# Four blocks for batch 0, swapped operands for the last 192 tokens, and output rows of 2 KB in a fused Fourier-mixing and mixture-of-experts kernel

## The chip, the cores and the metric

One core of a Trainium2 chip (trn2). The metric is the time of one execution on the device in microseconds (us), lower is better. Each kernel is timed in several executions; a run of the kernel before stands in the same rounds on the same chip. All runs quoted are fast, with a mean granted TensorE clock of 0.99 to 1.00. A profile shows one single execution: for the changed kernels one of the timed ones, for the kernel before a further one.

## The reference

Eight batches of 2496 tokens with 256 channels pass through a Fourier mixing layer; then each batch goes as a whole to one of eight experts.

```python
X = np.fft.rfft(x, axis=1)                     # x: 8 x 2496 x 256
Yr = Xr @ w_r - Xi @ w_i + b_r                 # complex 256x256 mixing
Yi = Xr @ w_i + Xi @ w_r + b_i
Y  = soft_threshold(Yr, 0.01) + 1j * soft_threshold(Yi, 0.01)
y  = np.fft.irfft(Y, n=2496, axis=1)
# mixture of experts, one expert e for a whole batch
e   = argmax(y.mean(axis=1) @ w_gate)
out = gate_weight * (np.maximum(y @ w1[e], 0) @ w2[e])   # 256 -> 1024 -> 256
```

## The kernel before

The transform of 2496 = 39 x 64 points is done by matmuls in two steps. A token index is 64 a + n, with a below 39 and n below 64. Everything is issued in a fixed order: a small list scheduler written in Python runs while the kernel is built. It takes operations in order of a priority `vt` and of its own estimates of durations and arrivals, and emits each to its engine. Every engine of the chip is thus given its list in a fixed order. So an estimate or a priority never delays anything by itself, but it decides what stands in front of what.

Cuts marked with `# ...`:

```python
class Schedule:
    def mm(self, cols, emit, vt, deps=(), allocs=(), after=None): ...   # a TensorE op
    def evac(self, n, emit, vt, deps=(), allocs=()): ...  # PSUM eviction: ScalarE or VectorE, chosen by the scheduler
    # an op waits for deps and for the earlier users of the buffers in allocs

apool = pool("ap", 1)             # ONE buffer for the tile A
opool = pool("op", 4)             # output tiles, 128 x 2 x 256 fp32
BANKS = {"a": 4, "h": 2, "o": 2}  # PSUM banks

# batch 0: its spectrum V is built inside the A buffer, then turned by TensorE in six pieces
VTk = S.tok("A", 1)
def add_turn(v_ops, vt):
    for gq in range(6):
        # ...  8 matmuls against an identity, out of the A buffer
        m = S.mm([128] * (2 * len(gs)), mm, vt(0.8 + 0.02 * gq), ...)
        VTk.rel.append(m)         # A is free after the last turn matmul
        # ...  one eviction of 1024 columns

# batches 2 to 7: the first step of the forward transform also writes A
Ak = S.tok("A", 1)
m = S.mm([512], mm, vt(-0.2 + 0.01 * gp), ..., allocs=[tk] if gp else [tk, Ak])
# ... then A -> DRAM -> XB (a transposing round trip), and the mixing starts from XB

# batch 0: inverse in six pieces, all of them needed by the first MoE matmul
for gb in range(6):
    va = vt(0.9 + 0.02 * gb)
    # ...  8 matmuls, one eviction of 936 columns into ysb

NCH = [(0, 512), (512, 512), (1024, 512), (1536, 512), (2048, 448)]
def add_moe(b, y_ops, yk, gate):
    for c, (ns, nl) in enumerate(NCH):
        for fc in range(E):       # 8 pieces of the hidden layer
            # two matmuls of nl columns, then a relu eviction of nl columns
            m = S.mm([nl, nl], mm, v, deps=y_ops + [w], ...)
        for sp in range(2):       # two pairs of output tiles, each 128 tokens x 256
            s0 = min((2 * sp + i) * P, nl - P)   # the last tile of 448 overlaps by 64
            nc.tensor.matmul(oc["p"][:, i, :],               # 16 per pair
                             cell["hs"][:, ft, s0 : s0 + P],   # tokens are the weights
                             w2s_t[b][:, ft, :], ...)          # 256 columns move
            # eviction with the gate's scale, store on the sync queue in rows of 1 KB
```

The first four chunks of batch 7 use a Strassen product; the change does not touch it.

Of the kernel before, what the change touches and what calls it, by code (L numbers as in the profile page):

```python
# [11 lines left out]
FP32 = mybir.dt.float32  # L12
# [23 lines left out]
def _tables():  # L36
# [22 lines left out]
    wi = wi.reshape(6, NK1, 117)  # L59
    wi0 = wi.transpose(1, 0, 2).reshape(120, 117)  # L60
    wi = np.concatenate([wi[:, k0:k9].reshape(-1, 117) for k0, k9 in PARTS])
# [74 lines left out]
class Schedule:  # L136
# [60 lines left out]
    def run(self):  # L197
        free = dict.fromkeys(("PE", "ACT", "DVE", "SP", "POOL"), 1.3)
        free["PE"], free["ACT"], free["SP"], free["POOL"] = 3.85, 4.0, 3.5, 6.0
        ring = {"SP": 17.5, "POOL": 26.0}  # L200
        todo = sorted(self.ops, key=lambda o: o.vt)
# [47 lines left out]
def kernel(  # L249
# [114 lines left out]

    X0_AT, X1_AT = (5.2, 7.6, 9.4, 10.8), 26.5
    W_AT = 11.6
    TF_AT, TI_AT = (12.3, 14.4, 16.4), (13.2, 15.4, 17.4)

# [9 lines left out]
    WARM, COLD, WARM_END = 60, 12, 11.9  # L378
    LATE = -0.12
    FAST = {(B - 1, c) for c in range(4)}  # L380
# [130 lines left out]
    def add_inverse_b(b, q, cell, oy, vt, wide):  # L511
# [38 lines left out]
        return o  # L550

    VTk = S.tok("A", 1)
    S.preset(VTk)
# [41 lines left out]
    def add_turn(v_ops, vt):  # L595

        V2k = S.tok("V2", 2)
        t_ops = []
        for gq in range(6):
            gs = range(4 * gq, min(4 * gq + 4, NG))  # L600
            tag = "oh"[gq % 2]
            tk = S.tok(tag, BANKS[tag], 2)
            hc = {}

            def mm(_, gq=gq, gs=gs, tag=tag, hc=hc):
                if gq == 0:
                    V2_t[0] = v2pool.tile([120, NG, D], FP16, name="V2")
                hc["p"] = pair(tag)
                pt = hc["p"].rearrange("p h c -> p (h c)")
                for i, g in enumerate(gs):  # L610
                    for ch in range(2):
                        c0 = D * i + P * ch
                        nc.tensor.matmul(  # L613
                            pt[0:120, c0 : c0 + P],
                            first["T"][:, ch, g], eye)
            m = S.mm([128] * (2 * len(gs)), mm, vt(0.8 + 0.02 * gq),
                     deps=v_ops + [small], after=t_ops[-1] if t_ops else None,
                     allocs=[tk] if gq else [tk, V2k])
            VTk.rel.append(m)

            def ev(eng, gs=gs, hc=hc):
                n = len(gs)
                src = hc["p"].rearrange("p h c -> p (h c)")
                COPY[eng](out=V2_t[0][:, gs[0] : gs[0] + n].rearrange(
                    "p g c -> p (g c)"), in_=src[0:120, 0 : D * n])
            e = S.evac(D * len(gs), ev, vt(0.8 + 0.02 * gq), deps=[m])
            tk.rel.append(e)
            t_ops.append(e)
        return t_ops, V2k
# [322 lines left out]
    def add_inverse_a(b, v_ops, vt):  # L952
# [31 lines left out]
        if b == 0:  # L984
            yk, y_ops = S.tok("ysb", 2), []
            for gb in range(6):
# [4 lines left out]
                def mm(_, gs=gs, cell=cell):  # L991
                    if gs[0] == 0:
                        ysb_t[b] = ypool.tile([P, 2, N], FP16, name="ysb")
                    cell["p"] = pi = pair("a")
                    for ch in range(2):
                        for i, g in enumerate(gs):
                            M = 39 if g == 21 else 117
                            nc.tensor.matmul(
                                pi[:, ch, 117 * i : 117 * i + M],
                                V2_t[0][:, g, ch * P : ch * P + P],  # L1000
                                wi0[:, 0:117:3] if g == 21 else wi0)
                cols = ([117] * len(gs) if gb < 5 else [117, 39]) * 2
                va = vt(0.9 + 0.02 * gb)
                m = S.mm(cols, mm, va, deps=[r_ops[gb]],
# [4 lines left out]
                def ev(eng, gb=gb, cell=cell):  # L1009
                    yv = ysb_t[b].rearrange("p h (a n) -> p h a n", n=N2)  # L1010
                    nf = 4 if gb < 5 else 1
                    pi = cell["p"]
                    COPY[eng](  # L1013
                        out=yv[:, :, :, 12 * gb : 12 * gb + 3 * nf].rearrange(
                            "p h a (g j) -> p h a g j", j=3),
                        in_=pi[:, :, 0 : 117 * nf].rearrange(
                            "p h (g a j) -> p h a g j", g=nf, j=3))
                    if gb == 5:
                        COPY[eng](out=yv[:, :, :, 63], in_=pi[:, :, 117:156])
                e = S.evac(936 if gb < 5 else 480, ev, va, deps=[m])  # L1020
                tk.rel.append(e)
# [4 lines left out]
        for gb in range(6):  # L1026
            gs = range(4 * gb, min(4 * gb + 4, NG))
            for ch in range(2):
# [3 lines left out]
                def mm(_, gs=gs, ch=ch, cell=cell):  # L1032
# [4 lines left out]
                    for i, g in enumerate(gs):  # L1037
# [7 lines left out]
                va = (vt(0.9 + 0.02 * gb) if b < 1  # L1045
                      else (b + LATE + 0.01 * gb) * PERIOD)
                m = S.mm(cols, mm, va,
# [102 lines left out]

    NCH = [(0, 512), (512, 512), (1024, 512), (1536, 512), (2048, 448)]

# [123 lines left out]
    T_t = {}  # L1276

    def add_moe(b, y_ops, yk, gate):
        w, gb_op, wk = gate
        v0 = b * PERIOD  # L1280
        if any(x == b for x, _ in FAST):
            t_op = add_weight_sums(b, w, wk, v0 - 0.05 * PERIOD)
        for c, (ns, nl) in enumerate(NCH):
            hk = S.tok("hs", BUFS["hs"])
            cell = {}
            h_ops = []
            for fc in range(E):
                v = v0 + PERIOD * (c * 8 + fc) / 44
                tag = "h" if b < B - 1 else "a"
# [3 lines left out]
                def mm(_, fc=fc, ns=ns, nl=nl, cell=cell, hc=hc, tag=tag):  # L1293
# [5 lines left out]
                    for ch in range(2):  # L1299
# [3 lines left out]
                            start=(ch == 0), stop=(ch == 1))  # L1303
                m = S.mm([nl, nl], mm, v, deps=y_ops + [w], after=m if fc else None,
                         allocs=[tk] if fc else [tk, hk])
# [12 lines left out]
            if (b, c) in FAST:  # L1318
                add_fast(b, c, ns, nl, cell, h_ops, hk, wk, t_op, gb_op, v0)
                continue  # L1320
            for sp in range(2):
                tago = "o" if b < B - 1 else "h"
                ok = S.tok(tago, BANKS[tago])
                last = b == B - 1 and c == 4 and sp == 1
                ok2 = S.tok(tago, BANKS[tago])
                oc = {}
                for q in range(4):
                    v = v0 + PERIOD * (c * 8 + 6 + 4 * sp + q) / 44

                    def mm(_, sp=sp, q=q, nl=nl, cell=cell, oc=oc, tag=tago,  # L1330
                           last=last):
                        if q == 0 or q == 2 and last:
                            oc["p"] = oc["p", q // 2] = bank(tag).rearrange("p (i c) -> p i c", i=2)
                        i = q // 2
                        s0 = min((2 * sp + i) * P, nl - P)
                        for ft in range(4 * (q % 2), 4 * (q % 2) + 4):
                            nc.tensor.matmul(  # L1337
                                oc["p"][:, i, :],
                                cell["hs"][:, ft, s0 : s0 + P],
                                w2s_t[b][:, ft, :],  # L1340
# [9 lines left out]

                def ev(eng, oc=oc):
                    oc["o"] = ost = opool.tile([P, 2, D], FP32, name="ost")
                    if eng == "ACT":
                        nc.scalar.activation(out=ost, in_=oc["p"],  # L1354
                                             func=AFT.Copy, scale=gbc_t[b])
                    else:
                        nc.vector.tensor_scalar_mul(out=ost, in0=oc["p"],
                                                    scalar1=gbc_t[b])

                def st(_, ns=ns, nl=nl, sp=sp, oc=oc):  # L1360
                    ost = oc["o"]
                    r0 = ns + 256 * sp
                    if 256 * sp + 256 <= nl:
                        nc.sync.dma_start(
                            out=out[b, r0 : r0 + 256, :].rearrange(
                                "(i p) c -> p i c", p=P),
                            in_=ost)
                    else:
                        nc.sync.dma_start(out=out[b, r0 : r0 + P, :],
                                          in_=ost[:, 0, :])  # L1370
                        nc.sync.dma_start(out=out[b, r0 + P : ns + nl, :],
                                          in_=ost[64:P, 1, :])

                def ev_last(_, ns=ns, nl=nl, sp=sp, oc=oc):
# [3 lines left out]
                    nc.scalar.activation(  # L1378
                        out=ost[64:P, 1], in_=oc["p", 1][64:P, 1],
                        func=AFT.Copy, scale=gbc_t[b][64:P])  # L1380
                    nc.scalar.dma_start(out=out[b, r0 + P : ns + nl, :],
                                        in_=ost[64:P, 1, :])

                def ev_first(_, ns=ns, sp=sp, oc=oc):
# [3 lines left out]
                        out=ost[:, 0], in0=oc["p", 0][:, 0], scalar1=gbc_t[b])  # L1388
                    nc.sync.dma_start(out=out[b, r0 : r0 + P, :],
                                      in_=ost[:, 0, :])  # L1390
                if last:
# [4 lines left out]
                else:  # L1396
                    e = S.evac(560, ev, v, deps=[m2, gb_op])
                    ok.rel.append(e)
                    S.op("SP", 0.3, st, v, deps=[e], dma=0.75)

# [34 lines left out]
```

## Time and profile before

| | before |
|---|---|
| time | 434.88 us median (434.28 to 435.47) |
| span of the profile | 433.1 us |
| matmul work in it (columns/2.4 GHz + 2.5 ns for each matmul) | 408.1 us |
| idle TensorE up to 50 us / from 60 to 150 us | 18.9 us / 0.5 us |
| end of the last matmul / from there to the end of the span | 429.3 us / 3.8 us |

The page of the kernel before, its head, its DMA queues and its chain of waits:

```profile
span 433.1 us, 9390 instructions
PE 419.6 (97%) x3553; PEld 312.2 (72%) x3553; DVE 300.8 (69%) x614; ACT 333.0 (77%) x643; POOL 35.4 (8%) x57
...
q1 hardware_dynamic: 68262, 57.41, 48.3%
q0 software_dynamic: 17216, 18.70, 28.5%
...
PE 89%; DMA 5%; ACT 3%; POOL 1%; SPq 1%; issue 0%; DVE 0%; ACTq 0%; POOLq 0%
```

PE is TensorE, and it holds 89% of the chain. Its busy time is a union of spans whose ends are modelled, so a full slice can still hide small waits. This document therefore also counts work: for every matmul record its columns divided by 2.4 GHz, plus 2.5 ns. The Trainium skill, "TensorE: Matmul & The Clock Gate", section "Back-to-back issue gap", gives N/2.4 + 2.5 ns as the gap of a warm, isolated matmul of N columns. The trace agrees with it for matmuls in a stream too: 109 ns from start to start at 256 columns, 216 ns at 512. "Idle" below is elapsed time less the work of all matmuls started so far, without the warm-up dummies. It contains the wait for the first data, and it would contain time at a lower clock. The last matmul is taken to end one such gap after its start, 0.1 us before its modelled end in the trace.

The stretches view of the kernel before (start:end, length, then busy us and count for each engine, granted clock, DMA share, GB/s):

```profile
31.00:50.00 19.00, 17.04 (x193) 12.73 (x194) 15.85 (x26) 17.78 (x30) 0.00 (x0) 1.00 0.73 103
60.00:70.00 10.00, 10.00 (x66) 6.46 (x65) 6.58 (x12) 8.62 (x17) 0.00 (x0) 1.00 0.76 229
70.00:80.00 10.00, 10.00 (x78) 7.25 (x76) 4.43 (x7) 7.86 (x16) 0.00 (x0) 1.00 1.08 257
80.00:90.00 10.00, 10.00 (x86) 7.74 (x84) 8.02 (x23) 7.06 (x15) 2.45 (x4) 1.00 0.76 157
100.00:150.00 50.00, 50.00 (x420) 38.14 (x418) 38.88 (x79) 38.57 (x78) 4.22 (x6) 1.00 0.89 207
```

From 60 us on TensorE (first number after the length) is full. From 31 to 50 us it shows 17.04 of 19, and the matmuls started there hold only 14.9 us of work; ScalarE (fourth) is busy 17.78. The start is where time is lost. Of 2.3 us of TensorE waits that the profile lists from 25 to 50 us, 2.0 name ScalarE or VectorE, so evictions limit it for the most part.

The chain of waits, one place that returns with the period of a batch:

```profile
187.09 0.46 PE ps L527 x4
...
237.23 0.46 PE ps L527 x4
```

One batch takes 50.14 us. Of the lines, L613 holds the turn matmuls of batch 0 and L793 forward matmuls, those of batch 2 among them. The last turn matmul frees the A buffer that L793 then writes:

```profile
42.33 0.39 PE L613 MATMUL ps<-eye,A 128*120 128x128 f16 x4
...
45.54 0.38 PE L793 MATMUL ps<-xin,wa 117*120 117x512 f16 x1 [0.43 <-ACT ysb L1013]
...
62.50 0.38 PE L793 MATMUL ps<-xin,wa 117*120 117x512 f16 x1
```

And the end of the span:

```profile
425.67 3.77 PE L1337 MATMUL ps<-w2s,hs 128*128 128x256 f16 x32
...
429.47 0.47 ACT L1378 ACTIVATE ost<-ps,gbc 64x256 f32<-64x256 f32 x1 [1.12 <-PE ps L1337]
429.97 0.55 ACTq L1381 DMA_DIRECT2D out_dram<-ost  x1
```

The last store is issued by 430.52 and the span ends at 433.1: 2.6 us for that store to land.

### The profile page before, as it was taken

The page shows a single profiled execution, that of the slowest core. Times are in us where ns is not written, and L with a number is a line of the kernel's source. Part 1 is how long each engine was busy: PE and PEld are TensorE (multiplying, and loading weights), DVE is VectorE, ACT ScalarE, POOL GpSimd, SP SyncE. Part 2 cuts the span into 40 slices and gives each one's busy share as a digit, 9 for nine tenths or more (in the row PEclk, how much of TensorE's full clock was granted, in tenths as well). Part 3 has the DMA queues.
Part 4 walks back from the last instruction along what each step waited for, and adds up shares of the span by engine and source line. Part 5 has one row for each costly group of instructions (what it writes and reads, how often), then busy time and mean ns, then how long its engine had stood idle before and what let it go on. Part 6 is the DMA issues. An engine that isn't in the chain of part 4 may idle for free.

```text
span 433.1 us, 9390 instructions
## 1 busy us (share of the span) xinstructions
PE 419.6 (97%) x3553; PEld 312.2 (72%) x3553; DVE 300.8 (69%) x614; ACT 333.0 (77%) x643; POOL 35.4 (8%) x57
## 2 busy tenths in 40 slices
PE   5888999999999999999999999999999999999996
PEld 2456567778777877778777877778777787777775
DVE  1488866577977787786977878777877869513561
ACT  3789987688876877678867888678777788678884
POOL 5230100011002000021001100020000010000000
PEclk9999999999999999999999999999999999999999
DMA  8899197999895997879995998959987285521122
GB/s 153 224 181 148 33 248 230 200 174 206 208 280 121 226 197 206 248 140 239 180 243 183 194 205 214 284 103 226 207 215 236 87 160 129 182 88 68 50 99 92
DMA packets 85785, 76.96 MB, mean 178 GB/s; under 512 B 7673, under 2 KB 72695, under 8 KB 85740
## 3 DMA queue, kind: packets, MB, share of 16 engines
q1 hardware_dynamic: 68262, 57.41, 48.3%
q0 software_dynamic: 17216, 18.70, 28.5%
q8 instruction: 28, 0.46, 0.5%
q10 hardware_dynamic: 262, 0.25, 0.2%
q14 instruction: 17, 0.14, 0.1%
HBM read 57.54 MB, written 37.49 MB: 219 GB/s over the span
## 4 chain that ended last, share of the span: by engine, by line
PE 89%; DMA 5%; ACT 3%; POOL 1%; SPq 1%; issue 0%; DVE 0%; ACTq 0%; POOLq 0%
PE ps L1300 30%; PE ps L1337 29%; PE ps L895 9%; DMA xin<-in_x_dram 4%; PE ps L1040 4%; PE ps L527 3%; PE ps L793 3%; PE ps L857 3%; PE ps L1219 2%; PE ps L699 2%; ACT hs L1312 1%; DMA tf<-d_tf 1%; PE ps L613 1%; PE ps L732 0%; POOL xin L321 0%
## 5 line engine op out<-in xcount | busy, mean ns | idle before, releaser
L1312 ACT ACTIVATE hs<-ps 128x512 f16<-128x512 f32 (+1 forms) x293 | 168.2, 594 | 68.6 <-PE ps L1300 64.7
L1300 PE MATMUL ps<-ysb,w1s 128*128 128x512 f16 (+1 forms) x640 | 178.4, 374 | 0.1
L1337 PE MATMUL ps<-w2s,hs 128*128 128x256 f16 x1152 | 162.4, 272 | 0.1
L1337 PEld LDWEIGHTS <-hs 128*128 128x128 f16 x1152 | 110.8, 98 | 42.7 <-issue 0.2
L1300 PEld LDWEIGHTS <-w1s 128*128 128x128 f16 x640 | 68.6, 113 | 18.8 <-issue 0.6
L909 DVE TENSOR_TENSOR tt<-ps,bias 128x512 f16<-128x512 f32 x60 | 38.6, 686 | 24.5 <-PE ps L895 24.5
L937 DVE TENSOR_TENSOR Y<-z,cl 64x512 f16<-64x512 f16 x120 | 50.4, 420 | 2.8
L895 PE MATMUL ps<-w,XT 128*128 128x256 f16 x360 | 49.4, 273 | 0.0
L1354 ACT ACTIVATE ost<-ps,gbc 128x512 f32<-128x512 f32 x65 | 44.8, 689 | 2.3 <-PE ps L1337 2.3
L895 PEld LDWEIGHTS <-XT 128*128 128x128 f16 x360 | 35.2, 98 | 7.7
L918 DVE TENSOR_TENSOR z<-ps,tt 128x512 f16<-128x512 f32 x60 | 38.4, 681 | 0.1
L803 ACT CAST A<-ps 120x512 f16<-120x512 f32 x48 | 29.5, 614 | 7.0 <-PE ps L793 6.6
L1056 DVE CAST ysb<-ps 128x468 f16<-128x468 f32 (+1 forms) x24 | 15.0, 629 | 25.6 <-PE ps L1040 25.5
L1056 ACT CAST ysb<-ps 128x468 f16<-128x468 f32 (+1 forms) x60 | 28.0, 523 | 3.2 <-PE ps L1040 2.6
L865 DVE CAST XT<-ps 128x512 f16<-128x512 f32 x24 | 16.5, 688 | 16.0 <-PE ps L857 16.0
L534 ACT CAST V<-ps 128x512 f16<-128x512 f32 x44 | 25.7, 609 | 0.0
L793 PE MATMUL ps<-xin,wa 117*120 117x512 f16 x66 | 23.1, 380 | 0.4 <-ACT ysb L1013 0.4
L534 DVE CAST V<-ps 128x512 f16<-128x512 f32 x26 | 17.9, 688 | 6.5 <-PE ps L527 5.4
L1040 PE MATMUL ps<-wi,V 120*128 120x117 f16 (+1 forms) x308 | 22.4, 214 | 0.0
L865 ACT CAST XT<-ps 128x512 f16<-128x512 f32 x36 | 22.0, 615 | 0.0
L527 PE MATMUL ps<-Y,ti 128*128 128x256 f16 x140 | 21.8, 272 | 0.0
L1040 PEld LDWEIGHTS <-V 120*128 120x128 f16 x308 | 19.8, 98 | 2.4
(104 smaller groups left out, 415.0 us busy)
## 6 DMA issues: line engine op xcount, KB each, us to landing
out_dram<-ost SPq DMA_DIRECT2D x72, 256.0 KB
xin<-in_x_dram POOLq DMA_DIRECT2D x21, 429.0 KB, 11.3
scr<-V SPq DMA_DIRECT2D x35, 256.0 KB
XB<-fwd SPq DMA_DIRECT2D x30, 256.0 KB
V<-scr SPq DMA_DIRECT2D x14, 504.0 KB
fwd<-A SPq DMA_DIRECT2D x18, 360.0 KB
w1s<-in_moe_w_dram POOLq DMA_DIRECT2D x8, 512.0 KB, 7.1
w2s<-in_moe_w_dram POOLq DMA_DIRECT2D x8, 512.0 KB, 8.9
```

The costliest lines, as they stand in the source:

```text
L534: COPY[eng](out=hc["V"][:, n * u : n * u + n].rearrange("p i c -> p (i c)"), in_=hc["p", u])
L865: COPY[eng](out=cell["X"][:, ch, :, 0:2].rearrange("p a r i k -> p a i r k"), in_=hc["p"].rearrange("p (a i r k) -> p a i r k", a=2, i=2, ...
L895: nc.tensor.matmul(pm[:, D * a : D * a + D], cell["X"][:, ch, a, t].rearrange("p i k -> p (i k)"), w4[:, ch, t, :], start=(ch == 0), stop= ...
L909: nc.vector.tensor_add(out=cell["tt"][:, r], in0=cell["T", 2].rearrange("p (a c) -> p a c", a=2), in1=bias[:, r].unsqueeze(1).to_broadcast ...
L918: nc.vector.tensor_add(out=cell["z"][:, r], in0=cell["T", 1 - r].rearrange("p (a c) -> p a c", a=2), in1=cell["tt"][:, r])
L937: nc.vector.tensor_sub(out=Y[64 * r : 64 * r + 64, :, i], in0=cell["z"][s, r], in1=cell["cl"][s, r])
L1040: nc.tensor.matmul(pi[:, 117 * i : 117 * i + M], V2[:, g, ch * P : ch * P + P], w)
L1056: COPY[eng](out=yv[:, :, 12 * gb : 12 * gb + 3 * nf].rearrange("p a (g j) -> p a g j", j=3), in_=pi[:, 0 : 117 * nf].rearrange("p (g a j) ...
L1300: nc.tensor.matmul(ph[:, 0:nl], w1v[:, ch, fc // 4, :, fc % 4], ysb_t[b][:, ch, ns : ns + nl], start=(ch == 0), stop=(ch == 1))
L1312: nc.scalar.activation(out=o, in_=i, func=AFT.Relu)
L1337: nc.tensor.matmul(oc["p"][:, i, :], cell["hs"][:, ft, s0 : s0 + P], w2s_t[b][:, ft, :], start=(ft == 0), stop=(ft == E - 1))
L1354: nc.scalar.activation(out=ost, in_=oc["p"], func=AFT.Copy, scale=gbc_t[b])
```

## The change

Its intents: start batch 0's MoE before its whole inverse transform is done; save the 64 tokens that are computed twice in each last chunk; write longer rows to memory.

1. Batch 0's tokens are laid out in four blocks of 16 values of n. MoE on the first block needs two of the six inverse pieces. The later pieces, and the turn pieces that feed them, are deferred.
2. The last 192 tokens of batches 1 to 7 are computed with operands swapped: w2 is the weight, 192 token columns move. The result is channel by token, so VectorE transposes it in 32 x 32 squares, and GpSimd (the queue that also casts inputs) stores it in rows of 256 B.
3. Output tiles take alternate tokens, so that two neighbouring tokens (2 KB) lie in one partition.
4. New expected arrival times, and an earlier priority for batch 1's inverse (`LATE1`).

```diff
-    X0_AT, X1_AT = (5.2, 7.6, 9.4, 10.8), 26.5
+    X0_AT, X1_AT = (5.2, 8.4, 10.0, 11.35), 30.5          # and others of this kind
-    LATE = -0.12
+    LATE, LATE1 = -0.12, -0.4
+    Y_AT = {2: 2.0, 3: 9.0, 4: 16.0, 5: 20.0}
@@ add_turn
-            m = S.mm([128] * (2 * len(gs)), mm, vt(0.8 + 0.02 * gq),
+            va = vt(0.8 + 0.02 * gq) if gq < 2 else Y_AT[gq] - 1.5
+            m = S.mm([128] * (2 * len(gs)), mm, va,
@@ inverse of batch 0
-                va = vt(0.9 + 0.02 * gb)
+                va = vt(0.9 + 0.02 * gb) if gb < 2 else Y_AT[gb]
@@ chunks: start, length, tiles as (start, tokens per partition), 0 = swapped
-    NCH = [(0, 512), (512, 512), (1024, 512), (1536, 512), (2048, 448)]
+    YB = 16 * N1
+    Y_NEED = {0: 2, 1: 3, 2: 4, 3: 6}
+    NCH0 = [c for r in range(4) for c in (
+        (YB * r, 256, ((0, 2),)), (YB * r + 256, 368, ((0, 2), (240, 1))))]
+    NCH = [(512 * c, 512, ((0, 2), (256, 2))) for c in range(4)] + [
+        (2048, 448, ((0, 2), (256, 0)))]
@@ add_turned (new)
+                    nc.tensor.matmul(
+                        oc["p"][:, h],
+                        w2s_t[b][:, ft].rearrange("p (m h) -> p h m", h=2)[:, h],
+                        cell["hs"][:, ft, s0:nl], ...)
+        e = S.evac(2 * n, ev, v, deps=[m, gb_op])
+            nc.vector.transpose(...)
+            for q in range(4):
+                nc.gpsimd.dma_start(out=ov[q], in_=...)      # rows of 64 fp32
@@ add_moe
+            order = [*enumerate(tiles)]
+            if b == B - 1 and c == 4:
+                order = order[::-1]
+            for sp, tile_s in order:
+                if not tile_s[1]:
+                    add_turned(..., v0 + PERIOD * (x + 6 * nl / 512 + 4 * sp) / 44)
+                    continue
...
-                                cell["hs"][:, ft, s0 : s0 + P],
+                                cell["hs"][:, ft, slice(s0 + i, s0 + n * P, n)],
-                                "(i p) c -> p i c", p=P),
+                                "(p i) c -> p i c", i=2),
```

## The prediction

> **What bounds it now.** Per slice, TensorE is busy without a gap from 50 to 422 us (stretches view: 50.00 of 50.00 in every period); the chain of waits is 89% TensorE, and one batch takes 50.14 us (the same chain entry returns at 137.87, 188.01, 238.15, 288.29). Busy matmuls overlap their modelled ends, so I count columns in the time order of matmuls: columns/2.4 GHz plus 2.5 ns each (the Trainium skill, "TensorE: Matmul & The Clock Gate", part 2, gives N/2.4+2.5 ns; the trace agrees: 109 ns at 256 columns, 217 at 512). That gives 49.7 us of matmul in each 50 us of steady state, but only 13.9 us in 12–31 us and 14.9 us in 31–50 us: about 9 us of lost TensorE time, all at the start. In 30–50 us ScalarE is busy 18.8 of 20 and VectorE 16.8: evictions limit there. Batch 0's first MoE matmul waits for all six pieces of its inverse transform and starts at 46.3 us. DMA is 90% busy in the steady state, but no TensorE wait there names it.
>
> **The change.**
> 1. Swapped tail, batches 1–7: two tiles of 128 tokens (64 computed twice) cost 16 matmuls x 109 = 1.74 us; now 16 of 192 columns at 82.5 ns = 1.32. Gain 0.42 us a batch, 3.0 us in all, fully on the critical path in batches 1–6. Extra: an eviction of 384 columns (0.55 us), a VectorE transpose of 384 fp32 columns (estimate 0.55 us), four GpSimd issues (about 0.7 us each, as the weight loads' 0.73–0.76). VectorE has 11 us free per 50 us, GpSimd far more: hidden.
> 2. Weights read with a step of two for all output tiles. The step-of-four loads of w1s take 113 ns against 98; the 120-column loads of eye transposes take 133 ns and still sustain one matmul per 55 ns. So loads stay hidden: 0 us.
> 3. 2 KB rows: on the sync queue packets of 1024 B average 51 ns, 2048 B 98 ns: nearly no byte rate gained, and DMA is not what TensorE waits for: 0 us. The 768 packets of 256 B per batch are small.
> 4. Batch 0 in four blocks: MoE may start after two of six pieces, about 39–41 us instead of 46.3, putting matmul-rich MoE work (33.7 us matmul to about 30 us eviction) in place of batch 1's eviction-rich transform. Of the 4 us lost in 31–50 I expect 2 back. Cost: 24 more relu evictions, each with about 0.15 us fixed time, on two engines that have room after 55 us; extra matmul overhead 0.1 us. The corrected arrival times only reorder: 0.3 us.
> 5. Tail: the swapped tile of batch 7 is stored by four GpSimd DMAs after eviction and transpose. Last store issue moves from about 430 to 430.5–431 us, plus landing: +0.5 us, against the 0.42 gained.
>
> **Sum.** 434.8 - 3.0 - 2.3 + 0.5 = 430.0 us; range 427.0 to 433.0 (8 in 10). Chances: faster by over 2% 0.10, within 2% 0.87, slower 0.03.
>
> **What would show it.** Period 49.7 instead of 50.14; swapped matmuls about 82 ns apart, other output matmuls still 109; first MoE matmul of batch 0 near 40 us and matmul work in 31–50 near 17 us; the chain ending in a GpSimd store; no TensorE wait on DMA in the middle.
>
> **What would make it wrong.** Step-of-two weight loads paced above 109 ns (up to +4 us); the 256 B stores holding output buffers behind the casting loads, stalling ScalarE; the late pieces of batch 0 holding batch 2's first buffer, so that a gap opens near 80–100 us; or the early start recovering all 4 us instead of 2.

## The result

438.5 us (437.67 to 439.45, four runs) against 434.88 for the kernel before. A ratio in this document is the mean time of one kernel's fast runs over that of the other's of the same rounds, so it is not quite the ratio of the quoted medians. Here it is 1.0084, 95% interval 1.0059 to 1.0109: slower by 0.8%, and outside the predicted range.

The page after; the groups here are the new stores on GpSimd:

```profile
span 437.1 us, 9564 instructions
PE 418.5 (96%) x3602; PEld 315.3 (72%) x3602; DVE 306.4 (70%) x636; ACT 335.4 (77%) x655; POOL 51.0 (12%) x85
...
q1 hardware_dynamic: 58690, 55.96, 44.9%
q0 software_dynamic: 18112, 20.08, 30.2%
...
PE 83%; DMA 6%; DVE 3%; ACT 3%; POOL 1%; issue 1%; SPq 1%; POOLq 0%; DVEq 0%
...
L1333 POOL DMA_DIRECT2D out_dram<-ost x28 | 16.1, 583 | 75.3 <-DVE ost L1321 74.4
```

The hardware queue sends 9,572 packets fewer, and TensorE's share of the chain drops from 89 to 83%. The stretches after, the same cuts as before:

```profile
31.00:50.00 19.00, 17.29 (x202) 14.06 (x201) 16.57 (x24) 15.67 (x29) 0.00 (x0) 1.00 0.62 97
60.00:70.00 10.00, 9.75 (x75) 7.41 (x74) 5.67 (x10) 7.95 (x17) 0.00 (x0) 1.00 0.47 141
70.00:80.00 10.00, 9.75 (x78) 7.66 (x77) 5.59 (x10) 8.68 (x22) 0.00 (x0) 1.00 1.12 221
80.00:90.00 10.00, 9.21 (x105) 7.82 (x104) 4.51 (x9) 7.88 (x19) 2.45 (x4) 1.00 1.00 295
100.00:150.00 50.00, 49.62 (x390) 36.77 (x388) 39.86 (x88) 37.60 (x73) 4.70 (x7) 1.00 0.84 205
```

TensorE is no longer full from 60 to 150 us, although VectorE (third number) is busy only 4.5 to 5.7 of 10 us from 60 to 90. The waits of TensorE between 60 and 150 us (who waited for whom: us in total, times, longest) are short, and none names the A buffer (those for `hs` are waits for a PSUM bank of the hidden layer to be evicted):

```profile
PE ps L1362 <- ACT hs L1375: 0.5, 2, 0.3
PE ps L1041 <- DMA out_dram<-ost: 0.4, 1, 0.4
PE ps L1362 <- DVE hs L1377: 0.4, 1, 0.4
PE ps L1094 <- DVE tt L911: 0.2, 1, 0.2
```

The chain of waits at the place shown before:

```profile
188.52 0.46 PE ps L527 x4
...
238.44 0.46 PE ps L527 x4
```

The period is 49.92 us, 0.22 less than before; the prediction said 49.7. Now the turn matmuls (L614 after) and the forward matmuls of batch 2 (L795 after):

```profile
71.76 0.39 PE L614 MATMUL ps<-eye,A 128*120 128x128 f16 x4
71.98 1.15 PE L795 MATMUL ps<-xin,wa 117*120 117x512 f16 x4
...
75.25 0.60 PE L795 MATMUL ps<-xin,wa 117*120 117x512 f16 x2
```

The last turn piece now runs at 71.76 us and the forward transform starts 0.22 us after it, 26 us later than before the change. The end:

```profile
428.24 1.48 PE L1296 MATMUL ps<-hs,w2s 128*128 128x192 f16 x16
...
429.76 0.58 ACT L1311 ACTIVATE ost<-ps,gbc 128x384 f32<-128x384 f32 x1 [1.07 <-PE ps L1296]
430.37 0.58 DVE L1321 STREAM_TRANSPOSE ost<-ost 128x384 f32<-128x384 f32 x1 [2.18 <-ACT ost L1311]
431.25 2.26 POOL L1333 DMA_DIRECT2D out_dram<-ost  x4 [31.15 <-DVE ost L1321]
```

The swapped tile is the last work of the kernel: eviction, transpose, then four stores until 433.51 us, and 3.6 us more until the span ends.

The difference of the two spans, 4.0 us, splits as follows (work and idle counted as above, from the matmul records of the two traces):

| term | before | after | difference | predicted |
|---|---|---|---|---|
| matmul work | 408.05 | 405.19 | -2.9 | -3.0, plus 0.1 of overhead |
| idle up to 50 us | 18.89 | 16.66 | -2.2 | -2.3 |
| idle 50 to 60 us | 0.03 | 0.29 | +0.3 | 0 |
| idle 60 to 150 us | 0.51 | 3.99 | +3.5 | 0 |
| idle 150 us to the last matmul | 1.79 | 3.43 | +1.6 | 0 |
| last matmul to the end of the span | 3.83 | 7.54 | +3.7 | +0.5 |

Both gains came as predicted. Two losses, of 3.5 and 3.7 us, ate them; a third, of 1.6 us in small pieces after 150 us, took back over half of the saved work.

### The profile page after: what moved, and what is told of

Same layout as the page of the kernel before. It is cut to its first block, busy times and chain, and to the rows that moved or that the text cites. A ratio compares the mean times of both kernels' runs of the same rounds, so it can differ in the third digit from the quotient of the medians.

```text
span 437.1 us, 9564 instructions
## 1 busy us (share of the span) xinstructions
PE 418.5 (96%) x3602; PEld 315.3 (72%) x3602; DVE 306.4 (70%) x636; ACT 335.4 (77%) x655; POOL 51.0 (12%) x85
## 4 chain that ended last, share of the span: by engine, by line
PE 83%; DMA 6%; DVE 3%; ACT 3%; POOL 1%; issue 1%; SPq 1%; POOLq 0%; DVEq 0%
PE ps L1362 29%; PE ps L1410 24%; PE ps L897 8%; DMA xin<-in_x_dram 4%; PE ps L527 4%; PE ps L1041 3%; PE ps L795 3%; PE ps L859 3%; PE ps L1225 3%; PE ps L701 2%; PE ps L1296 2%; ACT hs L1375 1%; DMA out_dram<-ost 1%; DMA tf<-d_tf 1%; DVE Y L939 1%
## 5 line engine op out<-in xcount | busy, mean ns | idle before, releaser
L1375 ACT ACTIVATE hs<-ps 128x512 f16<-128x512 f32 (+3 forms) x318 | 173.7, 565 | 65.7 <-PE ps L1362 61.8
L1362 PE MATMUL ps<-ysb,w1s 128*128 128x512 f16 (+3 forms) x688 | 180.7, 359 | 1.1 <-ACT hs L1375 0.5
L1410 PE MATMUL ps<-w2s,hs 128*128 128x256 f16 x1040 | 149.5, 272 | 0.0
L1410 PEld LDWEIGHTS <-hs 128*128 128x128 f16 x1040 | 100.7, 98 | 39.4 <-issue 1.0
L1362 PEld LDWEIGHTS <-w1s 128*128 128x128 f16 x688 | 73.6, 113 | 19.0 <-issue 2.6
L911 DVE TENSOR_TENSOR tt<-ps,bias 128x512 f16<-128x512 f32 x60 | 38.7, 686 | 17.2 <-PE ps L897 16.9
L1427 ACT ACTIVATE ost<-ps,gbc 128x512 f32<-128x512 f32 (+1 forms) x55 | 36.7, 670 | 2.4 <-PE ps L1410 1.6
L805 ACT CAST A<-ps 120x512 f16<-120x512 f32 x42 | 23.5, 616 | 2.6 <-PE ps L795 2.5
L1057 ACT CAST ysb<-ps 128x468 f16<-128x468 f32 (+1 forms) x50 | 23.0, 530 | 2.8 <-PE ps L1041 2.6
L1333 POOL DMA_DIRECT2D out_dram<-ost x28 | 16.1, 583 | 75.3 <-DVE ost L1321 74.4
L795 PE MATMUL ps<-xin,wa 117*120 117x512 f16 x66 | 22.3, 380 | 0.0
L1377 DVE TENSOR_SCALAR hs<-ps 128x512 f16<-128x512 f32 (+3 forms) x26 | 15.3, 595 | 9.8 <-PE ps L1362 8.5
```

Source lines behind the costliest of these rows:

```text
L795: nc.tensor.matmul(pa[0:120, :], wa, xin_t[b][:, gp, 0 : 2 * D])
L911: nc.vector.tensor_add(out=cell["tt"][:, r], in0=cell["T", 2].rearrange("p (a c) -> p a c", a=2), in1=bias[:, r].unsqueeze(1).to_broadcast ...
L1057: COPY[eng](out=yv[:, :, 12 * gb : 12 * gb + 3 * nf].rearrange("p a (g j) -> p a g j", j=3), in_=pi[:, 0 : 117 * nf].rearrange("p (g a j) ...
L1362: nc.tensor.matmul(ph[:, 0:nl], w1v[:, ch, fc // 4, :, fc % 4], ysb_t[b][:, ch, ns : ns + nl], start=(ch == 0), stop=(ch == 1))
L1375: nc.scalar.activation(out=o, in_=i, func=AFT.Relu)
L1410: nc.tensor.matmul(oc["p"][:, i, :], cell["hs"][:, ft, ts], w2s_t[b][:, ft, :], start=(ft == 0), stop=(ft == E - 1))
```

## The experiments

Two theories. First, the swapped tile at the very end costs 3.7 us because a longer chain follows the last matmul. Second, deferring the turn pieces keeps the only A buffer until 72 us, so batch 2 has no mixing work ready for TensorE between 60 and 90 us. In the trace, the first matmul that reads batch 2's XB, the start of its mixing, comes at 78.8 us before the change and at 88.7 us after it. The rivals: small chunks and their evictions; the moved priority; step-two weights and longer rows; the new arrival times.

Every run keeps the scheduler, so each edit may also reorder other instructions. The table gives the quantities that the readings rest on, each from the run's profile. "Before" was 434.6 to 435.4.

| run | median us | ratio to before | batch 2 forward, first start | idle to 50 | idle 60-150 | last matmul ends | from there to the end |
|---|---|---|---|---|---|---|---|
| before | 434.88 | | 45.5 | 18.9 | 0.5 | 429.3 | 3.8 |
| the change | 438.50 | 1.0084 | 72.0 | 16.7 | 4.0 | 429.6 | 7.5 |
| e1_tail_plain | 435.79 | 1.0028 | 71.7 | 16.4 | 4.0 | 430.3 | 3.9 |
| e2_tail_first | 437.70 | 1.0071 | 71.5 | 16.2 | 4.1 | 429.6 | 6.4 |
| e9_hw_store | 436.43 | 1.0036 | 72.0 | 16.7 | 3.9 | 429.4 | 5.1 |
| e3_two_A | 436.38 | 1.0049 | 46.9 | 16.1 | 1.9 | 426.5 | 7.5 |
| e15_two_A_held | 438.66 | 1.0088 | 72.1 | 16.8 | 3.9 | 430.4 | 7.7 |
| e4_turn_early | 436.02 | 1.0029 | 47.8 | 17.1 | 1.5 | 427.1 | 7.5 |
| e8_two_A_plain_tail | 433.38 | 0.9964 | 47.1 | 16.2 | 1.8 | 427.1 | 3.8 |
| e17_turn_early_plain_tail | 433.93 | 0.9969 | 47.6 | 17.0 | 1.3 | 427.4 | 3.8 |
| e6_b0_old | 438.28 | 1.0090 | 47.1 | 17.9 | 2.1 | 427.9 | 8.1 |
| e7_before_times | 434.19 | 0.9979 | 47.1 | 17.9 | 0.6 | 428.6 | 3.8 |
| e14_swap_only | 435.47 | 1.0032 | 47.7 | 18.5 | 1.9 | 428.9 | 3.5 |
| e11_no_swap | 434.82 | 0.9994 | 47.6 | 16.7 | 1.8 | 429.6 | 3.5 |
| e12_halves | 437.94 | 1.0076 | 49.3 | 16.0 | 6.4 | 431.4 | 3.9 |
| e13_halves_late | 441.04 | 1.0143 | 50.1 | 16.9 | 9.1 | 435.8 | 3.9 |
| e5_late_old | 433.67 | 0.9970 | 48.7 | 17.8 | 2.4 | 429.1 | 3.8 |
| e16_rows_1k_mended | 433.65 | 0.9967 | 48.2 | 17.3 | 2.3 | 429.2 | 3.8 |

Repeats of one kernel spread over 1 to 3 us, so a difference under about 0.7 us between two medians is not read. The columns from the fourth on come from one execution each, which can be the fastest of its run (e14) or the slowest (e15, e5). Some of these executions hold a wait that others lack: the traces of e1 and e15 have one or two of 0.6 to 1.0 us for a batch's input after 250 us. So small differences between traces are not read either.

### The end: ordinary tiles (e1_tail_plain)

```diff
-            if b == B - 1 and c == 4: order = order[::-1]
+            if b == B - 1 and c == 4: tiles = ((0, 2), (192, 2))   # 64 tokens twice, stored once
```

> The changed kernel, but batch 7's last 448 tokens are two ordinary tiles again (the second of them computes 64 tokens twice and is stored by the two hardware queues); nothing else differs. Theory (the swapped tile is the last thing to end, and its chain of eviction, transpose, four GpSimd issues and landing took 7.5 us after the last matmul against 3.8 us before): the end of the span comes about 3.7 us nearer to the last matmul, which itself moves 0.4 us later; time 438.5 - 3.3 = 435.2 us. Rival (the lost time is all earlier, the end is only where it shows): under 1 us gained, 437.5 or more.

435.79 us. The tail after the last matmul is back at 3.9 us, 2.7 us gained in the median. The theory's mechanism holds; its 3.3 us was a little too much. The loss at the end is a cause of its own.

### The end: swapped tile first (e2_tail_first)

```diff
-                             after=m2 if q else None,
+                             after=m2 if q else (last swapped matmul if b == B - 1 else None),
```

> The changed kernel, but in batch 7 the swapped tile's matmuls are forced ahead of the ordinary tile's, as the reversed list in the change seems to intend (its priorities undo it). The slow chain then starts about 1.3-1.7 us earlier and runs beside the last ordinary tile. Theory (length of the swapped chain): 436.5 to 437.2, thus some 1.5 us gained but not the 3.3 of the plain tail, because the four issues and the landing still end last. Rival (only the order was wrong, not the length): as good as the plain tail, 435.2.

437.70 us, worse than either statement. The swapped matmuls do run first, and the stores are issued 1.66 us sooner, but the span still ends with them. The time order of this run:

```profile
426.54 1.48 PE L1296 MATMUL ps<-hs,w2s 128*128 128x192 f16 x16
...
427.86 1.92 PE L1413 MATMUL ps<-w2s,hs 128*128 128x256 f16 x16
428.11 0.58 ACT L1312 ACTIVATE ost<-ps,gbc 128x384 f32<-128x384 f32 x1 [1.62 <-PE ps L1296]
...
429.59 2.26 POOL L1334 DMA_DIRECT2D out_dram<-ost  x4 [29.18 <-DVE ost L1322]
```

The stores are out at 431.85 and the span ends at 436.0, 4.15 us later. So the order was not the whole fault: the swapped chain is longer than the ordinary tile that follows it.

### The end: hardware queues (e9_hw_store)

```diff
-                nc.gpsimd.dma_start(...)
+                eng = nc.gpsimd if b < B - 1 else (nc.sync, nc.scalar)[q % 2]
+                eng.dma_start(...)
```

> The changed kernel, but the four stores of batch 7's swapped tile go out from the two hardware queues (two each) in place of GpSimd; eviction and transpose stay. Theory A (the GpSimd queue is the slow part of the tail: 0.3 us to start, 2.26 us for four issues, 3.6 us to land): the span ends 5.0 to 5.5 us after the last matmul in place of 7.5, time 436.2 to 436.7. Theory B (the 256 B pieces and the extra transpose are the slow part, whoever issues): 437.5 or more.

436.43 us: theory A. The same four stores leave two queues in 0.86 us, in place of 2.26 on one:

```profile
430.21 0.58 DVE L1321 STREAM_TRANSPOSE ost<-ost 128x384 f32<-128x384 f32 x1 [2.18 <-ACT ost L1311]
430.81 0.82 SPq L1334 DMA_DIRECT2D out_dram<-ost  x2
430.82 0.86 ACTq L1334 DMA_DIRECT2D out_dram<-ost  x2
```

They land by 434.5, 2.8 us after the last issue, although the two hardware queues moved them as 768 packets of 256 B and GpSimd as 64 packets of 3072 B. So small packets were not what made the end slow. Of the 3.7 us that the end lost, 2.4 (7.5 less 5.1) belong to issuing all four stores from the GpSimd queue; the run changed the kind of queue and their number at once, and does not part the two. What remains is mostly the longer chain before it.

### The middle: a second A buffer (e3_two_A)

```diff
-    apool = pool("ap", 1);  VTk = S.tok("A", 1);  Ak = S.tok("A", 1)
+    apool = pool("ap", 2);  VTk = S.tok("A", 2);  Ak = S.tok("A", 2)
-    spool = pool("sp", 1)        # 10 KB for batch 7's sums
+    # batch 7's sums are put into an A buffer, to make room
```

> The changed kernel with a second buffer for the tile A (room made by putting the last batch's sums into the same ring). In the changed kernel the deferred turn pieces of batch 0 keep the only A buffer until about 72 us, and batch 2's forward transform (72-75 us, before the change 45-63 us) and its way through memory come late. Theory (late A buffer starves TensorE between 60 and 150 us, 3.7 us lost there): forward transform of batch 2 back before 65 us, idle from 60 to 150 us down from 4.0 to 1 us or less, time 438.5 - 3 = 435.5. Rival (the smaller blocks' evictions and two banks limit there): idle stays near 4 us, time 437.5 to 438.5.

436.38 us. Batch 2's forward transform starts at 46.9 us, the idle from 60 to 150 us falls from 4.0 to 1.9, and the last matmul ends 3.1 us earlier. The stretches of this run:

```profile
60.00:70.00 10.00, 10.00 (x75) 7.28 (x73) 6.22 (x12) 8.35 (x18) 0.00 (x0) 1.00 0.93 260
70.00:80.00 10.00, 9.50 (x91) 8.16 (x90) 6.83 (x12) 7.80 (x17) 0.00 (x0) 1.00 1.06 249
80.00:90.00 10.00, 9.99 (x115) 8.61 (x113) 8.88 (x26) 8.63 (x20) 2.46 (x4) 1.00 0.67 175
100.00:150.00 50.00, 50.00 (x419) 38.01 (x417) 37.86 (x78) 38.09 (x73) 4.77 (x7) 1.00 0.88 208
```

Against the change, 80 to 90 us fills from 9.21 to 9.99 and VectorE rises from 4.51 to 8.88: batch 2's mixing has arrived (its first matmul at 73.7 us). The 4.0 did not fall to the 1 us expected; 1.9 remains. By stretches, the idle of 80 to 110 us falls from 2.5 to 0.5, and the 1.1 us of 60 to 80 us stay as they were: the late transform does not explain those.

### The middle: the second buffer, but batch 2 held back (e15_two_A_held)

```diff
-                     after=m if gp else None,
+                     after=m if gp else TURN[-1] if b == 2 else None,   # on top of e3_two_A
```

> The run with two A buffers, but batch 2's first forward matmul is ordered behind batch 0's last turn piece, as the single buffer forced it; the second buffer, and the memory moved for it, stay. Theory (the late forward transform of batch 2 is what starves TensorE): forward transform again from about 72 us, idle of 60-150 us back at 3.5 us or more (4.0 in the changed kernel, 1.9 with two buffers), time 438 to 438.6. Rival (something else that came with the second buffer gave the 2.1 us): idle stays near 2 us, 436.4.

438.66 us, idle 3.9 us, forward transform from 72.1 us, mixing from 88.5 us. The stretch from 80 to 90 us, where the second buffer had 9.99 on TensorE and 8.88 on VectorE:

```profile
80.00:90.00 10.00, 9.39 (x107) 7.99 (x105) 4.53 (x10) 8.04 (x20) 2.47 (x4) 1.00 1.02 294
```

With the memory of the second buffer but the order of one buffer, the whole 2.1 us that it gained is lost again. It is the lateness of batch 2's transform, and not something else that the second buffer brought.

### The middle: one buffer, early turn (e4_turn_early)

```diff
-            va = vt(0.8 + 0.02 * gq) if gq < 2 else Y_AT[gq] - 1.5
+            va = vt(0.8 + 0.02 * gq)
```

> The changed kernel with one A buffer, but all six turn pieces of batch 0 at their old priority, so that A is free early; only the later pieces of the inverse stay deferred. Theory (as above): forward transform of batch 2 before 65 us, idle of 60-150 us 2 us or less; the four evictions of turn pieces of 1.03 us on ScalarE (1.2 on VectorE) come before the first MoE matmuls, so 0.5 to 1.5 us of the start goes back; time 436.5 to 437.5. Rival: idle of 60-150 us stays near 4 us and the time is 438.5 or more.

436.02 us, idle 1.5 us, forward transform from 47.8 us, mixing from 75.3 us. The same stretch here:

```profile
80.00:90.00 10.00, 9.63 (x99) 8.22 (x98) 8.81 (x24) 7.55 (x18) 0.74 (x2) 1.00 0.75 204
```

The same cause removed from the other side: with a single buffer, releasing it early is enough. The expected price at the start hardly came: the first MoE matmul stays at 41.2 us, and 0.4 us more is idle by 50 us.

### Both repairs (e8_two_A_plain_tail, e17_turn_early_plain_tail)

> The changed kernel with both repairs at once: a second buffer for A and ordinary tiles at the end of batch 7. Theory (two independent causes, one between 60 and 150 us and one after the last matmul): the gains add, 438.5 - 2.1 - 2.7 = 433.7 us, ratio to the kernel before about 0.998. Rival (both act on the same slack): no better than the better of the two, 435.8.

433.38 us (432.5 to 435.38), ratio 0.9964 with interval 0.9936 to 0.9992. The gains add: 438.5 - 2.1 - 2.7 = 433.7.

> The simple repair: the changed kernel with the six turn pieces at their old priority (one A buffer, as there) and ordinary tiles at the end of batch 7. If the two gains add here too: 436.0 - 2.7 = 433.3 us, level with the version that needs a second buffer (433.4), and ahead of the kernel before. If the second buffer buys more than the early turn: 434 or more.

433.93 us in rounds in which the kernel before took 435.41, ratio 0.9969 with interval 0.9945 to 0.9993. This needs no second buffer, and by ratio it is level with the other. Both beat both kernels, by 0.3 to 0.4% over the kernel before: a small gain, with intervals just clear of 1. The new arrival times alone, in the kernel before (e7 below), reach 0.9979; the lead of the repaired versions over that is not resolved.

### The price of the swap (e11_no_swap)

```diff
-        (2048, 448, ((0, 2), (256, 0)))]
+        (2048, 448, ((0, 2), (192, 2)))]         # on top of e8
```

> The kernel with both repairs, but no swapped tiles at all: batches 1 to 6 also end in two ordinary tiles that overlap by 64 tokens. It prices the swap in the steady state, where the prediction had 0.42 us a batch and the traces show the period 50.14 turn into 49.91, 0.23 us a batch. By the period: 6 x 0.23 = 1.4 us slower than with the swap, 435.1. By the prediction's arithmetic: 2.5 us slower, 436.2. If the swapped tiles cost elsewhere (waits on output buffers or VectorE): no slower or faster, 433.7 or less.

434.82 us, 1.4 us slower than with the swap, nearer to the 1.4 of the period than to the 2.5 us of the arithmetic. But the agreement is in part luck: this run's own period is 50.23 us, so without the swap a batch takes 0.31 us longer, 1.9 us in six, and the two profiled spans differ by 2.1 us. The price lies between the two statements. The work returns in full (408.2 against 405.6 us), but idle from 150 us to the last matmul is 2.8 us without the swap and 3.2 with it. So a part of the saved work is given back as small waits in a fixed order. Which engine owes them was not settled; none exceeds 0.16 us in the repeating part of a period.

### Old batch 0 (e6_b0_old, e14_swap_only) and the arrival times alone (e7_before_times)

> The changed kernel with batch 0 and the early inverse of batch 1 as before the change: five chunks in natural token order, MoE after all six pieces, old priorities; the swapped tail, the 2 KB rows and the new arrival times stay (batch 0's last chunk is swapped too). Theory (blocks of batch 0 gain 2.2 us by 50 us and lose 3.7 us after): the idle before 50 us returns to about 18.9, that of 60-150 us falls under 1 us, time 438.5 - 1.9 = 436.6 (the long tail stays). Rival (the new arrival times or the swapped tiles cause the loss after 60 us): 438 or more, with the idle of 60-150 us still there.

438.28 us where 436.6 was expected: the forecast of the time failed. The idle before 50 us (17.9) and the early forward transform (47.1) are as the theory had them, and idle from 60 to 150 us falls to 2.1, not under 1. One wait makes half of it: 0.9 us at 102 us for batch 3's input. And the tail is 8.1 us: the transpose there waits 0.3 us longer, for an output buffer whose store has not landed. A new order brought new waits. Nor is all of the miss inside the span: the time was 2.4 us longer than the span in all four executions of this run, against 1.7 us in the kernel before of the same rounds, and these 0.7 us are not explained.

> The changed kernel with batch 0 in its old order (as in the earlier run of that kind) and ordinary tiles at the end of batch 7: so the swap in batches 0 to 6, the 2 KB rows and the new arrival times, without the four blocks and without the second A buffer. It prices the four blocks against the version with both repairs (433.4). By the cumulative idle of the traces (four blocks with a second A buffer are 0.6 us ahead of the kernel before at 150 us; this one lost 0.9 us on a wait for batch 3's input) it is within 0.7 us of 433.9. If the four blocks are worth their 2.2 us: 435.5 or more.

435.47 us with a spread from 434.21 to 438.59: neither within 0.7 us of 433.9 nor clearly above 435.5. Inconclusive as a price of the four blocks; the wait for batch 3's input is there again (0.8 us).

> The kernel before with nothing but the change's new arrival times (and ring times) in its scheduler. The prediction gave them 0.3 us. In the run with the old batch 0, which has them, the first MoE matmul starts at 44.5 us in place of 46.3 and the idle before 50 us is 17.9 in place of 18.9. Theory: the same here, 1.0 us less idle by 50 us, and with no other change the time 434.8 - 1.0 = 433.8. If the order is disturbed elsewhere: 434.5 or more.

434.19 us (434.13 to 434.27), ratio 0.9979 with interval 0.9955 to 1.0004. The idle before 50 us falls by 1.0 us and stays gained (idle up to the last matmul 20.5 against 21.2), about 0.7 us of the expected 1.0. So about 1.0 of the 2.2 us gained at the start came from the arrival times, not from the four blocks; the prediction had given them 0.3. That split is rough: the three traces with the arrival times and without the blocks gain 0.4 to 1.0 us.

### Fewer, larger chunks (e12_halves, e13_halves_late)

```diff
-    YB = 16 * N1        # four blocks, chunks of 256 and 368
+    YB = 32 * N1        # two blocks, chunks of 512, 512 and 224; on top of e8
     # ... Y_NEED, Y_AT, evictions and stores of batch 0 to match
```

> The kernel with both repairs, but batch 0 in two blocks of 1248 tokens (chunks of 512, 512 and 224) in place of four: 48 relu evictions instead of 64, the first MoE matmul after three of six pieces. Theory (what idle is left at 60-150 us, 1.9 us in the run with two A buffers, comes from the small chunks, whose matmul pair takes 0.31 us against 0.48 us for its eviction, with two banks): idle of 60-150 us 1 us or less, but the start gives 0.5 to 1 us back; time within 0.7 us of the four blocks. Rival (it is not the chunk size): idle of 60-150 us unchanged and a later start, 434.5 or more.

437.94 us. From 60 to 80 us the idle is 0.04 us where the four blocks with both repairs have 1.02: so this idle goes with the blocks, as the theory says. That it is the size of the chunks alone is not shown: the early-turn version has the same small chunks and 0.39 us there (e17). At 85.8 us TensorE stands for 3.76 us before batch 1's inverse, and the version loses. The stall costs more than its own length, as the granted clock (the third number from the right) shows:

```profile
80.00:90.00 10.00, 6.40 (x50) 4.57 (x48) 6.81 (x13) 3.94 (x7) 0.00 (x0) 0.96 0.79 192
90.00:100.00 10.00, 10.00 (x104) 8.18 (x102) 7.83 (x22) 7.82 (x17) 2.46 (x4) 0.87 0.86 144
```

In this trace the clock is 0.50 from 89.1 to 92.6 us, so the matmuls from the end of the stall at 89.8 us ran 2.8 us at half speed (213 ns from start to start at 256 columns, in place of 109). By an estimate from these numbers that lost 1.4 us, and it is counted in the idle of 6.4. In the traces of the kernel before and of the change the clock stays at 1.00 from 8 us to the last matmul.

> The two-block version, with batch 1's inverse transform back at its old priority (-0.12 periods in place of -0.4). In the two-block run TensorE stood 3.76 us at 85.8 us before batch 1's inverse, whose V tile had not landed. Theory (the early priority puts that matmul in the fixed order ahead of its data): the stall goes, idle of 60-150 us falls from 6.4 to 2 us or less, time 437.9 - 3.8 = 434.1 us or less. Rival (the data are late whatever the priority): idle unchanged, 437.5.

441.04 us. The stall at 85.8 us is gone, as expected, and a worse one takes its place: 7.35 us at 101.4 us before batch 3's forward matmul, whose input was issued at 90.5 us and had not landed. Here too the clock is 0.50, from 104.9 to 111.7 us, beyond the end of the stall. The time forecast failed outright.

### The moved priority of batch 1 (e5_late_old)

> The version with both repairs, but batch 1's inverse at its old priority (-0.12 periods). With two blocks this traded a wait of 3.76 us before batch 1's inverse for one of 7.35 us before batch 3's input. If batch 1's early inverse is what keeps batch 3's input in time: a wait on that input of 3 us or more near 100 us and 436 us or more. If that wait belonged to the two blocks alone: within 1 us of 433.4.

433.67 us, within 1 us: the wait for batch 3's input belonged to the two blocks alone. The profiled execution, the slowest of four, has a wait of 1.7 us for batch 1's input at the start instead. The priority `LATE1` is worth nothing that these runs resolve.

### Rows of 2 KB (e10_rows_1k, e16_rows_1k_mended)

```diff
+                        if 0 < b < B - 1: ts = slice(s0 + i * P, s0 + i * P + P)
-                                "(p i) c -> p i c", i=2),
+                                "(i p) c -> p i c", i=2),
```

> The version with both repairs, but batches 1 to 6 store tokens of consecutive rows again (1 KB pieces, weights of the output matmuls read without a step). The prediction gave the 2 KB rows and the step-two reads 0 us each: time within 0.5 us of 433.4, the same order of instructions, output matmuls 109 ns apart in both. If the 2 KB rows matter by relieving the DMA queues: 434.5 or more. If the step-two weight reads cost: 432.5 or less.

This run's result was wrong: batch 7 got the new store but kept alternate tokens, so 256 of its tokens came out in the wrong order. Its time, 433.74 us, is of the same instructions. The mended run keeps batch 7's store as in the change:

> The 1 KB rows again, mended: the first run stored the first 256 tokens of batch 7's last chunk in the wrong order and its result was wrong, its time 433.7. Expected as there: within 0.5 us of 433.4, the 2 KB rows and the step-two weight reads worth nothing either way.

433.65 us, ratio 0.9967 against 0.9964 with 2 KB rows. The rows and the step-two weight reads are worth nothing here, in either direction.

## Why the prediction was wrong

- **Swapped work: right.** It said 3.0 us less matmul work; the traces show 2.9, and the 16 swapped matmuls run 82.5 ns apart as computed. On the clock it was worth less: the period fell by 0.22 us and not by 0.42, and taking the swap out of the repaired kernel lengthened it by 0.31 us, 1.4 us in the time.
- **Step-two weights and 2 KB rows: right.** The loads take 98 ns as before, output matmuls stay 109 ns apart, and undoing the rows changes nothing. Its "768 packets of 256 B per batch" was wrong in form: from GpSimd the trace has 64 packets of 3072 B a batch.
- **Start: right in size, wrong in split.** It said 2.3 us; idle up to 50 us fell by 2.2, and the first MoE matmul came at 41.2 us where 39 to 41 was said. But about 1.0 us is due to the arrival times. Of the gain in matmul work, 1.0 us lies in 12 to 31 us and 1.35 us in 31 to 50 us, where it had 2 (16.3 us of work there, where it had said near 17).
- **The tail: the mis-sized term.** Point 5 said "Last store issue moves from about 430 to 430.5-431 us, plus landing: +0.5 us". The last issue ended at 433.51, and landing took 3.6 us in place of 2.6: 3.7 us in all. Two things are missing from its sum. The reversed list seems to put the swapped tile first, but its priority (`4 * sp` with sp = 1) puts it last; the prediction does not say which it assumed. And four issues of 0.57 us one after the other are 2.3 us, with nothing left to run beside. The order alone is little of it: with the swapped tile first, the median was only 0.8 us better.
- **The middle: the step that failed.** Point 4 took the 2 us gained at the start as kept, and costed only 24 more relu evictions "on two engines that have room after 55 us"; the buffer that the deferred turn pieces hold has no cost in the sum. It named "the late pieces of batch 0 holding batch 2's first buffer, so that a gap opens near 80-100 us" as a risk and gave it no number. The runs show that this is what happened: the last turn at 71.76 us, batch 2's transform 0.22 us behind it, and 3.5 us more idle from 60 to 150 us, of which 2.1 us go with a second buffer and 2.5 us with an early turn, and the 2.1 us return when the transform is held back. Two facts that warn of it were there before the run: the pool has one buffer (the source), and the transform that waits for it runs from 45.5 to 62.5 us (the trace).
- **What stays open.** After the repair 1.3 to 1.9 us of idle remain from 60 to 150 us, against 0.5 before. With a second buffer 1.0 us of it lies in 60 to 80 us and is gone in the two-block run; with an early turn it is 0.4 us; the rest, and the extra 1.6 us after 150 us, were not traced to one cause. Without the swap about 1.0 us of that 1.6 is still there, so the swap is not the whole of it.

The Trainium skill, "Perfetto Trace Analysis", section "Identifying Performance Opportunities" (its part on strategy), says of consistent bubbles on the engine that should be saturated that they "can mean there isn't enough SBUF/PSUM for the next tile to be allocated". This agrees in the cause, with a difference in the sign to look for: no bubble of the changed trace names the A buffer. The waits listed above name evictions, a DMA and a VectorE sum, at most 0.4 us each, and the lack of A shows only in when the forward matmuls and the mixing start.

## What to carry to other kernels

Before deferring an operation, list the buffers that it releases and who takes them next: deferring batch 0's turn pieces by 30 us cost 2.1 to 2.5 us, as much as the gain at the start, and one priority undid it. A slow store path can hide behind other work in the middle of a kernel and costs its whole length at the end, so give the last tile the path with the shortest way from matmul to memory, even if it computes more. In a fixed order of instructions, count the idle of the bounding engine stretch by stretch up to the end, because a gain early on is only real if it is still there at the last matmul.

## What the Trainium skill lacked or had wrong

- "TensorE: Matmul & The Clock Gate", "Back-to-back issue gap", says that in a stream of weight loads and matmuls the spacing is about 81 ns at N = 128 and 131 ns at N = 512, and calls N/2.4 + 2.5 ns the isolated gap. Here, with a weight load for every matmul, the stream runs at 56 ns at 128 columns, 82.5 ns at 192, 109 ns at 256 and 216 ns at 512: the formula holds, the sustained figures do not.
- The same page gives no cost for weights read with a step. Here loads of 128 columns of f16 took 98 ns on average with a step of one or two elements and 113 ns with a step of four, hidden under the matmuls in each case.
- "DMA: Bandwidth & Descriptors", "Specifications", tells the GpSimd and hardware paths apart by first-byte latencies of about 1 and 0.6 us. These are no measure of the end of a kernel, where issue and landing count: here four stores of 48 KB in rows of 256 B took 2.26 us to issue from GpSimd and landed 3.6 us after the last issue; from two hardware queues it was 0.86 us and 2.8 us.
- "VectorE: DVE Perf Modes", "The three transpose paths", has times for 128x128 bf16 only. Here 128x384 fp32 in 32 x 32 squares took 580 ns.
- No page consulted warns that work deferred in a static order also defers the release of its buffers: 2.1 to 2.5 us here, without one wait in the trace that names the buffer.
